# Attention and two mixture layers: the second half's products with v in two visits, three steps apart

## The chip, the cores and the metric

The kernel runs on one core of a Trainium2 chip. The core has a matrix engine (PE, which also loads its weights, PEld), a vector engine (DVE), a scalar engine (ACT), a general engine (POOL) and a queue that issues transfers (SP). Each takes its own instructions in the order in which they stand and waits for the others by semaphores. The metric is the device time of one execution in microseconds (us).

## The reference, cut to what matters

```python
def _attn_ref(q, k, v, tau):                 # 4 batches, 8 heads, 576 rows, 64 columns
    scores = scale * np.matmul(q, k.transpose(0, 1, 3, 2))
    thresh = np.max(scores, axis=-1, keepdims=True) - tau
    scores = np.where(scores >= thresh, scores, -1000000000.0)
    scores = scores - np.max(scores, axis=-1, keepdims=True)
    attn = np.exp(scores)
    attn = attn / (np.sum(attn, axis=-1, keepdims=True) + 1e-09)
    return np.matmul(attn, v)
# then h = x @ w_in, g = h * tanh(softplus(h)), x = g @ w_out      (2304 tokens, 512 -> 2048 -> 512)
# then a soft mixture of 8 experts with 4 slots each
```

The change lies in the attention alone, in its last product `attn @ v`.

## The kernel before, in words

The attention takes 16 pairs of heads, one after the other. A pair has two heads of 576 rows. Its rows come in nine chunks of 128: four of each head and a last one that holds the 64 rows left of both. The main loop runs over steps, one chunk each, so that step 9n+j works on chunk j of pair n; below, "step j" is a step of that place in any pair. PE, DVE and ACT are kept in one written order (`manual_schedule`), so that the place of a call in the loop is the place in the engine's queue.

In a step stand, in this order:

- PE, `emit_S`: the scores `s` of the chunk, 128 rows by 576 keys, four matmuls (eight in step 8, whose rows are of two heads). A score tile has two PSUM banks; there are three such tiles, so the scores of chunk i take the tile of chunk i-3 and wait for DVE to be done with that.
- PE, `emit_T`: four matmuls with the identity turn the masked exponentials `p` of the chunk three steps back (`T_LAG`), keys to the partitions, into a bank of `tp`. ACT copies the bank to `pT`. Of the name `tp` there are two banks, which the turns and the products with v share.
- DVE and ACT, `emit_E`: DVE finds the extreme `nm` of each row (its scores are negated), ACT takes the exponentials `e`.
- DVE, `emit_P`, for the chunk before: mask, product and row sum in one instruction; then `emit_th`, the next threshold.

Keys 512 to 575 are turned apart (`emit_R`, parts 0, 1 and 2 at the steps of `R_AT`): two small matmuls into the unused end of the step's score tile, ahead of the scores in PE's order; `evac_R` at the end of the step copies them to `pTr`.

A pair's product with v (`emit_V`) is done by halves of its rows: half 0 has 256 of each head, half 1 has 320. It is five key groups (kc 0 to 4) of two matmuls each, side by side in the two halves of PE's columns, summed in one bank of `tp`; kc 4 reads `pTr`. ACT then copies the bank to `xT`. `pv_at` places it: half 0 of pair n at the end of step 0 of pair n+1 (`PV_0`), half 1 at the end of step 4 of pair n+1 (`PV_1`).

Other work rides in the same loop. POOL splits the next pair's q and k. SP loads k, q and v two pairs ahead; v has three buffers. In pairs 1 to 12, three early weight tiles are unpacked: in every fourth pair (1, 5, 9) the step 4 holds an ACT instruction (`rebase`, L158), and the other parts are DVE instructions at the ends of steps 4 and 6 (`CONV`, `CVN`): one at step 6 in pairs 1, 5, 9; one at each of both steps in pairs 2, 3, 6, 7, 10, 11; one at step 4 in pairs 4, 8, 12. At step 4 of pairs 4, 8 and 12 a batch's row sums are turned too, and ACT copies them out (`rt`). At step 6 of pairs 12 to 15 ACT copies a part of the token block (`x_hi`). After the attention come the two mixture layers, which the change does not touch.

Of the kernel before, what the change touches and what calls it, by code (L numbers as in the profile page):

```python
# [8 lines left out]
F32 = mybir.dt.float32  # L9
# [15 lines left out]
NPR = B * NP  # L25
# [7 lines left out]


T_LAG = 3
PV_0 = 29
PV_1 = 14
R_AT = (6, 2, 3)
NORM_AT = (0, 4)
CONV = (4, 6, 13, 15, 22, 24, 31)  # L40
CVN = (9, 45, 81)
# [23 lines left out]
def pow2(n):  # L65

    return 1 << (n.bit_length() - 1)
# [3 lines left out]
def kernel(  # L71
# [21 lines left out]
    def copy_act(dst, src):  # L93
        act.activation(out=dst, in_=src, func=ACTF.Copy)  # L94
# [7 lines left out]
    tp = ctx.enter_context(tc.tile_pool(name="tp", bufs=2))  # L102
# [5 lines left out]
    ps_t = ph2.enter_context(tc.tile_pool(name="ps_t", bufs=2, space=PSUM))  # L108
# [75 lines left out]
    def spans(t0, n):  # L184
        a = t0
        while a < t0 + n:
            blk = a // BT
            e = min(t0 + n, (blk + 1) * BT)
            yield blk, a - blk * BT, a - t0, e - a
            a = e  # L190
# [194 lines left out]
            copy_act(tr[:64, 256:320], ps[:64, 0, :64])  # L385
            copy_act(tr[64:, 256:320], ps[64:, 1, 64:])

    def emit_V(n, half):

        b, hp = divmod(n, NP)  # L390
        w = 256 if half == 0 else 320
        t, tr = pT[n, half]
        vt, vrt = V[n]
        pv = ps_t.tile([128, 512], F32, name="tp")
        for kc in range(5):
            for h in range(2):
                hs = slice(64 * h, 64 * h + 64)
                lhsT, rhs = (vt[:, kc, h], t[:, kc, h]) if kc < 4 else (vrt[:, h], tr)
                pe.matmul(pv[hs, :w], lhsT=lhsT, rhs=rhs, start=(kc == 0), stop=(kc == 4))  # L399
        for blk, x0, p0, ln in spans(b * S + 256 * half, w):  # L400
            copy_act(xT[blk][:, hp, x0:x0 + ln], pv[:, p0:p0 + ln])

    def pv_at(i, z):

        n, k = divmod(3 * i + z, 27)
        for nn, half, place in ((n, 0, PV_0), (n - 1, 0, PV_0), (n - 1, 1, PV_1)):
            if place == k + 27 * (n - nn) - 27 * half and 0 <= nn < NPR:
                emit_V(nn, half)

    def norm_a(b):  # L410
        r = p1.tile([128, 36], F32, name="rr", bufs=2)
# [4 lines left out]
    def norm_b(b, i):  # L416
        o = SH if i < NCH else 0
        ps = st[i]["s"][:36, 0, o:o + 128]
        pe.transpose(ps, rinv[b], ident)
        return lambda: norm_out(b, ps)  # L420
# [80 lines left out]
    with tc.manual_schedule():  # L501
# [49 lines left out]
        for i in range(NCH + 9):  # L551
            n, j = divmod(i, 9)
            live = i < NCH
            if live or j in R_AT[1:]:
                st[i] = {"s": ps_s.tile([128, 2, 512], F32, name="s")}
            R = None
            pv_at(i, 0)
            if n < NPR and j == R_AT[0]:
                R = (n, 0, i)
            if n >= 1 and j in R_AT[1:]:  # L560
                R = (n - 1, R_AT.index(j), i)
            if R:
                emit_R(*R)
            turn_out = None
            if n >= 1 and (n - 1) % NP == NP - 1:
                if j == (NORM_AT[1] if n < NPR else R_AT[2]):
                    turn_out = norm_b((n - 1) // NP, i)
            if live:
                emit_S(i)
            pv_at(i, 1)  # L570
            if T_LAG <= i < NCH + T_LAG:
                emit_T(i - T_LAG)
# [4 lines left out]
            if live:  # L577
# [11 lines left out]
                for m in range(NWA):  # L589
# [3 lines left out]
                    if z in CONV:  # L593
                        cv[m][CONV.index(z)]()
                        if z == CONV[-1] and m + 1 < NWA:
                            early_w(m + 1)
            pv_at(i, 2)
            if n >= 1:
                m = n - 1
# [276 lines left out]
        for c0, w in COLS:  # L876
            n = pow2(1024 // w)
# [104 lines left out]
        for g in range(NF, NG, 2):  # L982
            blk, m = divmod(g, NF)
            prev = [g - 1] if g == NF else [g - 2, g - 1]
            plan = TRIPLES_0 if g == NF else TRIPLES_1 if m == 2 else TRIPLES
# [387 lines left out]
```

## Time and profile before

| | us |
|---|---|
| median of 3 runs (lowest to highest) | 755.63 (754.92 to 756.26) |
| the profiled execution | 755.94 |
| span of its instructions | 754.2 |
| PE busy | 728.1 (97%) |
| DVE busy | 519.9 (69%) |
| ACT busy | 459.1 (61%) |
| POOL busy | 391.9 (52%) |

The span runs from the first instruction to the last; 1.7 us of the execution lie around it. The shares are means over stages: the attention is the first 290 us, and there DVE and ACT are nearly as busy as PE. A busy PE is not PE at its peak, since the ends of matmuls are modelled; how long PE is kept by a group of instructions is read from the start of it to the start of the next.

### The profile page before, as it was taken

To read this page: it belongs to the slowest core of one execution; us is meant where nothing else is said; L and a number is where in the kernel's file an instruction comes from. 1 tells how busy PE (TensorE), PEld (TensorE's weight loads), DVE (VectorE), ACT (ScalarE), POOL (GpSimd) and SP (SyncE) were. 2 spreads that over 40 slices of the span, in tenths; PEclk is the share of its full clock that TensorE was granted. 3 is DMA by queue.
4 is the path that set the end of the run, shared out by engine and by line. 5 is a ranking of instruction groups with operands and counts; after the bars stand their busy time and mean duration, and the time that the engine had idled before them with its cause. 6 is when DMAs were issued, how large, how long until landed. Compare 5 with 4: busy or idle time off the path is not lost.

```text
span 754.2 us, 12760 instructions
## 1 busy us (share of the span) xinstructions
PE 728.1 (97%) x4641; PEld 596.0 (79%) x4641; DVE 519.9 (69%) x1018; ACT 459.1 (61%) x880; POOL 391.9 (52%) x395
## 2 busy tenths in 40 slices
PE   8999999999999999999999999999999999999995
PEld 6777777777777778998999888887898888898443
DVE  7888888888888883656986756568867545754413
ACT  6877787777777775444464655566646555644213
POOL 6665567666647733333645755465755454544000
PEclk8999999999999999999999999999999999999998
DMA  7422443433313203343330100000006111259798
GB/s 246 134 81 83 154 127 98 124 126 107 128 56 97 81 4 126 113 143 137 112 112 1 63 1 1 1 1 0 1 1 232 69 57 56 94 218 370 251 397 296
DMA packets 45678, 84.85 MB, mean 113 GB/s; under 512 B 6048, under 2 KB 21040, under 8 KB 45616
## 3 DMA queue, kind: packets, MB, share of 16 engines
q1 hardware_dynamic: 45344, 83.88, 32.8%
q8 instruction: 36, 0.59, 0.3%
q14 instruction: 26, 0.21, 0.1%
q10 hardware_dynamic: 272, 0.16, 0.1%
HBM read 79.23 MB, written 4.79 MB: 111 GB/s over the span
## 4 chain that ended last, share of the span: by engine, by line
PE 75%; DVE 13%; issue 6%; ACT 5%; DMA 1%; SPq 0%; POOL 0%; ACTq 0%
PE tp L399 11%; PE s L647 8%; PE s L649 8%; PE s L648 8%; DVE pab L340 7%; PE s L307 7%; PE tp L742 5%; PE tp L744 4%; PE tp L743 4%; PE tp L483 3%; PE tp L485 3%; PE tp L484 3%; PE tp L360 2%; PE hp L1195 2%; DVE nm L317 2%
## 5 line engine op out<-in xcount | busy, mean ns | idle before, releaser
L307 PE MATMUL s<-kb,Q 128*128 128x288 f32 (+2 forms) x672 | 126.0, 316 | 10.2 <-DVE pab L340 4.6
L317 DVE TENSOR_REDUCE nm<-s 128x1 f32<-128x576 f32 x144 | 108.0, 750 | 38.8 <-PE s L307 38.6
L307 PEld LDWEIGHTS s<-kb,Q 128*128 128x128 f32 x672 | 95.1, 192 | 37.0 <-DVE pab L340 15.5
L466 POOL TENSOR_TENSOR wo<-wr,wo 128x512 fp32r<-128x512 f32 x48 | 68.5, 1426 | 99.2 <-ACT wo L94 85.5
L318 ACT ACTIVATE e<-s,nm 128x576 f32<-128x576 f32 x144 | 106.5, 740 | 18.7 <-DVE nm L317 15.2
L647 PE MATMUL s<-wo,gg 128*128 128x512 f32 x288 | 115.8, 402 | 0.8 <-DVE big L657 0.7
L649 PE MATMUL s<-wo,gg 128*128 128x512 f32 x288 | 114.0, 396 | 0.0
L648 PE MATMUL s<-wo,gg 128*128 128x512 f32 x288 | 113.8, 395 | 0.0
L340 DVE SCALAR_TENSOR_TENSOR pab<-s,th,e 128x576 f32<-128x576 f32 x128 | 103.5, 808 | 1.7 <-ACT pTr L94 1.7
L94 ACT ACTIVATE pT<-tp 128x512 f32<-128x512 f32 x144 | 86.2, 598 | 24.6 <-PE tp L360 24.1
L360 PE MATMUL tp<-ident,pab 128*128 128x128 f32 x512 | 78.6, 276 | 0.1
L399 PE MATMUL tp<-pT,vt 128*64 128x320 f32 (+1 forms) x512 | 69.1, 412 | 0.4 <-ACT pT L94 0.3
L732 POOL TENSOR_TENSOR wi<-wr,wi 128x256 fp32r<-128x256 f32 x48 | 47.3, 986 | 41.6 <-ACT wi L94 41.5
L753 ACT ACTIVATE hs<-hs 128x384 f32<-128x384 f32 x64 | 33.4, 522 | 56.5 <-DVE hs L1031 35.7
L732 POOL TENSOR_TENSOR wi<-ev,wi 128x256 fp32r<-128x256 f32 x64 | 52.5, 831 | 23.8 <-ACT wi L94 23.8
L649 PEld LDWEIGHTS s<-wo,gg 128*128 128x128 f32 x288 | 54.4, 189 | 12.6
L360 PEld LDWEIGHTS tp<-ident,pab 128*128 128x128 f32 x512 | 62.2, 142 | 0.8 <-issue 0.7
L647 PEld LDWEIGHTS s<-wo,gg 128*128 128x128 f32 x288 | 54.5, 189 | 9.8 <-issue 1.8
L648 PEld LDWEIGHTS s<-wo,gg 128*128 128x128 f32 x288 | 54.6, 190 | 7.5 <-POOL wo L466 0.4
L756 DVE TENSOR_TENSOR gg<-hs,gg 128x384 fp32r<-128x384 f32 x64 | 54.5, 852 | 7.6 <-ACT gg L94 7.6
L91 POOL TENSOR_SCALAR kb<-kr,kscale 128x576 fp32r<-128x576 f32 x30 | 22.5, 750 | 61.6 <-PE s L307 61.6
L399 PEld LDWEIGHTS tp<-pT,vt 128*64 128x64 f32 x512 | 33.9, 136 | 24.9 <-issue 5.1
(284 smaller groups left out, 1572.0 us busy)
## 6 DMA issues: line engine op xcount, KB each, us to landing
kr<-in_k SPq DMA_DIRECT2D x32, 288.0 KB, 3.0
qr<-in_q SPq DMA_DIRECT2D x32, 288.0 KB, 3.2
big<-in_w SPq DMA_DIRECT2D x15, 512.0 KB, 7.1
wr<-in_w SPq DMA_DIRECT2D x14, 512.0 KB, 3.3
big<-in_w_in SPq DMA_DIRECT2D x10, 512.0 KB, 4.8
big<-in_w_out SPq DMA_DIRECT2D x10, 512.0 KB, 5.0
wr<-in_w SPq DMA_DIRECT2D x13, 352.0 KB, 8.3
big<-in_w SPq DMA_DIRECT2D x13, 320.0 KB, 6.9
```

The source lines that it names most:

```text
L94: act.activation(out=dst, in_=src, func=ACTF.Copy)
L307: pe.matmul(s[:, f, a:z], lhsT=t[:, o:o + 128], rhs=kb[:, hh, ko:ko + z - a], start=(j == 0), stop=(j == len(plan) - 1 and z == SH),)
L317: dve.tensor_reduce(out=nm, in_=s, axis=AX.XY, op=ALU.min)
L318: act.activation(out=e, in_=s, func=ACTF.Exp, bias=nm[:, 0:1], scale=-1.0)
L340: dve.scalar_tensor_tensor(out=p.rearrange("p (a b) -> p a b", a=2), in0=d["s"][:, :, :SH], scalar=d["th"][:, 0:1], in1=d["e"], op0=ALU.is ...
L360: pe.transpose(ps[:, kc], p[:, ko:ko + 128], ident)
L399: pe.matmul(pv[hs, :w], lhsT=lhsT, rhs=rhs, start=(kc == 0), stop=(kc == 4))
L466: pool.tensor_tensor(out=t[:, 1], in0=src, in1=t[:, 0].bitcast(F32), op=ALU.subtract)
L647: pe.matmul(ps, lhsT=hi[:, ts], rhs=w[:, 0], start=(m == 0), stop=False)
L648: pe.matmul(ps, lhsT=hi[:, ts], rhs=w[:, 1], start=False, stop=False)
L649: pe.matmul(ps, lhsT=lo[:, ts], rhs=w[:, 0], start=False, stop=(m == NF - 1))
L732: pool.tensor_tensor(out=lo, in0=src, in1=hi.bitcast(F32), op=ALU.subtract)
```

## The change

Half 0's product stays at step 0. Half 1's is now done in two visits: kc 0 and 1 at the end of step 3, kc 2, 3 and 4 at the end of step 6. In between the sum stays in its bank of `tp`. Part 2 of `emit_R`, which kc 4 needs, moves from step 3 to step 5. The counts and shapes of all instructions are the same.

```diff
 T_LAG = 3
-PV_0 = 29
-PV_1 = 14
-R_AT = (6, 2, 3)
+PV = ({29: (0, 1, 2, 3, 4)}, {38: (0, 1), 47: (2, 3, 4)})
+R_AT = (6, 2, 5)
...
-    def emit_V(n, half):
+    pvs = {}
+
+    def emit_V(n, half, kcs):
...
-        pv = ps_t.tile([128, 512], F32, name="tp")
-        for kc in range(5):
+        if kcs[0] == 0:
+            pvs[half] = ps_t.tile([128, 512], F32, name="tp")
+        pv = pvs[half]
+        for kc in kcs:
             for h in range(2):
...
                 pe.matmul(pv[hs, :w], lhsT=lhsT, rhs=rhs, start=(kc == 0), stop=(kc == 4))
+        if kcs[-1] < 4:
+            return
         for blk, x0, p0, ln in spans(b * S + 256 * half, w):
             copy_act(xT[blk][:, hp, x0:x0 + ln], pv[:, p0:p0 + ln])
...
-        for nn, half, place in ((n, 0, PV_0), (n - 1, 0, PV_0), (n - 1, 1, PV_1)):
-            if place == k + 27 * (n - nn) - 27 * half and 0 <= nn < NPR:
-                emit_V(nn, half)
+        for half, plan in enumerate(PV):
+            for back in range(2):
+                if k + 27 * back in plan and 0 <= n - back < NPR:
+                    emit_V(n - back, half, plan[k + 27 * back])
```

PE, steps 2 to 5 of the second pair before (`tp_953` is the bank of the product, the other `tp` those of turns, `s` with `pr` or `pab` the small turns of `emit_R`):

```order
L360 MATMUL tp_889<-ident_88,pr_108 128x128 x4
L377 MATMUL s_903<-ident_88,pr_108 128x128 x2
L307 MATMUL s_903<-kb_643,Q1_1_110 128x288 x2
L307 MATMUL s_903<-kb_643,Q2_1_112 128x288 x2
L360 MATMUL tp_912<-ident_88,pab_873 128x128 x4
L307 MATMUL s_931<-kb_643,Q1_1_110 128x288 x2
...
L360 MATMUL tp_936<-ident_88,pab_873 128x128 x4
L399 MATMUL tp_953<-pT1_779,vt_355 64x320 x8
L399 MATMUL tp_953<-pTr1_780,vrt_356 64x320 x2
L307 MATMUL s_965<-kb_643,Q1_1_110 128x288 x2
...
L360 MATMUL tp_970<-ident_88,pab_922 128x128 x4
```

PE, steps 3 to 7 of the same pair in the changed kernel, where `tp_927` is the product's bank:

```order
L359 MATMUL tp_910<-ident_88,pab_873 128x128 x4
L403 MATMUL tp_927<-pT1_779,vt_355 64x320 x4
L306 MATMUL s_932<-kb_643,Q1_1_110 128x288 x2
...
L359 MATMUL tp_937<-ident_88,pab_873 128x128 x4
L376 MATMUL s_954<-ident_88,pr_108 128x128 x2
...
L359 MATMUL tp_961<-ident_88,pab_920 128x128 x4
L374 MATMUL s_979<-ident_88,pab_873 128x128
...
L359 MATMUL tp_986<-ident_88,pab_920 128x128 x4
L403 MATMUL tp_927<-pT1_779,vt_355 64x320 x4
L403 MATMUL tp_927<-pTr1_780,vrt_356 64x320 x2
L306 MATMUL s_1008<-kb_643,Q1_1_110 128x288 x2
...
L359 MATMUL tp_1015<-ident_88,pab_971 128x128 x4
```

Eight matmuls and two stood together between two steps; now four stand behind the turn of step 3 and six behind that of step 6. Before, the turns go through the two banks by turns. In the changed kernel the product holds one bank from step 3 to step 6, and the five turns of steps 3 to 7 (`tp_910`, `tp_937`, `tp_961`, `tp_986`, `tp_1015`) are all placed in the other.

ACT, steps 3 to 5 of that pair before (`e` are the exponentials, `pT` the copies of turns, `big` the copy of the product):

```order
L94 ACTIVATE pT0_910<-tp_912 128x4x128
L318 ACTIVATE e_919<-s_903,nm_918 128x576
L94 ACTIVATE pTr1_780<-s_903 64x64 x2
L94 ACTIVATE pT0_910<-tp_936 128x4x128
L318 ACTIVATE e_943<-s_931,nm_942 128x576
L94 ACTIVATE big_105<-tp_953 128x320
L94 ACTIVATE pT0_910<-tp_970 128x4x128
L318 ACTIVATE e_977<-s_965,nm_976 128x576
```

ACT, steps 3 to 7 of that pair in the changed kernel:

```order
L93 ACTIVATE pT0_908<-tp_910 128x4x128
L317 ACTIVATE e_917<-s_903,nm_916 128x576
L93 ACTIVATE pT0_908<-tp_937 128x4x128
L317 ACTIVATE e_944<-s_932,nm_943 128x576
L93 ACTIVATE pT0_908<-tp_961 128x4x128
L317 ACTIVATE e_968<-s_954,nm_967 128x576
L93 ACTIVATE pTr1_780<-s_954 64x64 x2
L93 ACTIVATE pT0_908<-tp_986 128x4x128
L317 ACTIVATE e_993<-s_979,nm_992 128x576
L93 ACTIVATE big_105<-tp_927 128x320
L93 ACTIVATE pTr0_909<-s_979 128x256
L93 ACTIVATE pT1_1013<-tp_1015 128x4x128
```

The copy of part 2 (`pTr1_780`, 64x64) went from behind the exponentials of step 3 to behind those of step 5, the copy of the product from step 4 to step 6. Each copy of a turn still stands behind the exponentials of the step before.

## Rows read from the trace of the kernel before

**Rows 1.** Busy time by engine in the stretch of pairs 1 to 14; columns as printed.
```profile
core 0: us, PE busy (x) PEld busy (x) DVE busy (x) ACT busy (x) POOL busy (x), PEclk, DMA share, GB/s
21.70:264.22 242.52, 234.52 (x1743) 180.82 (x1741) 206.28 (x529) 186.63 (x355) 158.83 (x158) 1.00 0.34 108
```
**Rows 2.** Who waited for whom, same stretch: total us, times, longest us.
```profile
DVE nm L317 <- PE s L307: 35.1, 28, 1.7
```
**Rows 3.** Timeline (start us, us): first reduction of pairs 1 to 5 and 15.
```profile
21.70 0.75 DVE L317 TENSOR_REDUCE nm<-s 128x1 f32<-128x576 f32 x1
38.98 0.74 DVE L317 TENSOR_REDUCE nm<-s 128x1 f32<-128x576 f32 x1
56.45 0.75 DVE L317 TENSOR_REDUCE nm<-s 128x1 f32<-128x576 f32 x1
73.92 0.75 DVE L317 TENSOR_REDUCE nm<-s 128x1 f32<-128x576 f32 x1
90.83 0.75 DVE L317 TENSOR_REDUCE nm<-s 128x1 f32<-128x576 f32 x1
264.22 0.75 DVE L317 TENSOR_REDUCE nm<-s 128x1 f32<-128x576 f32 x1
```
**Rows 4.** Timeline of PE in pair 8, from half 0's product at step 0.
```profile
142.75 1.95 PE L399 MATMUL tp<-pT,vt 128*64 128x256 f32 x16
...
145.06 0.80 PE L307 MATMUL s<-kb,Q 128*128 128x288 f32 x4
145.70 0.60 PE L360 MATMUL tp<-ident,pab 128*128 128x128 f32 x4
146.13 0.38 PE L375 MATMUL s<-ident,pab 128*128 128x128 f32 x2
146.27 0.78 PE L307 MATMUL s<-kb,Q 128*128 128x288 f32 x4
...
147.44 0.44 PE L377 MATMUL s<-ident,pr 128*128 128x128 f32 x2
147.64 0.78 PE L307 MATMUL s<-kb,Q 128*128 128x288 f32 x4
...
149.63 0.60 PE L360 MATMUL tp<-ident,pab 128*128 128x128 f32 x4
150.16 2.37 PE L399 MATMUL tp<-pT,vt 128*64 128x320 f32 x16
...
153.00 0.80 PE L307 MATMUL s<-kb,Q 128*128 128x288 f32 x4
...
155.39 0.41 PE L307 MATMUL s<-kb,Q 128*128 128x288 f32 x1
```
**Rows 5.** Timeline of DVE in pair 8, at steps 1, 5 and 6.
```profile
145.90 0.76 DVE L317 TENSOR_REDUCE nm<-s 128x1 f32<-128x576 f32 x1 [0.69 <-PE s L307]
...
153.84 0.76 DVE L317 TENSOR_REDUCE nm<-s 128x1 f32<-128x576 f32 x1 [1.16 <-PE s L307]
154.52 0.81 DVE L340 SCALAR_TENSOR_TENSOR pab<-s,th,e 128x576 f32<-128x576 f32 x1
...
155.38 0.75 DVE L317 TENSOR_REDUCE nm<-s 128x1 f32<-128x576 f32 x1
```
**Rows 6.** Timeline of ACT in pair 8: a turn's copy, exponentials, small copies.
```profile
146.33 0.60 ACT L94 ACTIVATE pT<-tp 128x512 f32<-128x512 f32 x1 [0.71 <-PE tp L360]
146.83 0.73 ACT L318 ACTIVATE e<-s,nm 128x576 f32<-128x576 f32 x1
...
150.44 0.43 ACT L94 ACTIVATE pTr<-s 64x64 f32<-64x64 f32 x2
...
153.45 0.26 ACT L94 ACTIVATE rt<-s 36x128 f32<-36x128 f32 x1
```
**Rows 7.** Timeline of ACT: the weight tile's part in pair 5, `x_hi` in pair 15.
```profile
99.86 1.17 ACT L158 ACTIVATE big<-big 128x1024 f32<-128x1024 f32 x1
...
278.42 0.84 ACT L94 ACTIVATE big<-big 128x768 fp32r<-128x768 f32 x1
```

## The prediction

> **What bounds the kernel now.** I first read the windows view of pairs 1 to 14: in 242.52 us PE is busy for 234.52, DVE for 206.28, ACT for 186.63, at a granted clock of 1.00, the upper of PE's two levels, 2.4 GHz [rows 1]. All three are near the bound, so shares do not say which wait counts. The list of waits does: DVE waits 28 times, twice per pair, for scores, 35.1 us in all [rows 2], and those are the only long waits between PE and DVE. The timeline of one pair shows where: DVE stands still 0.69 us at step 1, behind half 0's product, and 1.16 us at step 5, behind half 1's [rows 5]. In the other steps DVE runs at 1.54 us from reduction to reduction (153.84 to 155.38 [rows 5]), and PE is the one held up: a step of scores and turn keeps PE about 1.07 us (0.63 + 0.44 below), but scores cannot run ahead by more than three tiles. So PE loses time before a product, and DVE loses it behind one. The length of a pair is the last fact needed: 17.28, 17.47, 17.47 and 16.91 us in pairs 1 to 4 [rows 3]; pairs 1, 2 and 3 carry a DVE part of a weight tile at step 6, pair 4 does not. So that part costs 0.37 (pair 1) or 0.56 us there, in full.
>
> **The times of PE, start to start** [rows 4]. Scores to turn 0.64 and 0.63 (I use 0.63; the scores of step 8, with twice the matmuls, 1.26). Turn to small turns 0.43, to a product 0.53, to scores 0.44 (estimate, from the 0.43). Small turns to scores 0.14, part 2 0.20. Half 0's product 2.31, half 1's 2.84: five key groups, 0.57 each, so the first visit is 1.14 and the second 1.70. From a score's start to its reduction 0.84 (153.00 [rows 4] to 153.84 [rows 5]). Scores of step i wait until the masking in step i-2 has ended: 1.55 behind the reduction there (153.84 to the score start at 155.39 [rows 4, 5]). On ACT: a turn's copy starts 0.63 behind the turn and takes 0.60; exponentials start 0.93 behind their reduction and take 0.73; the two small copies of part 2 take 0.43, the row sums' copy 0.26 [rows 4 to 6]. PE starts 0.06 behind what it waits for (masking from 154.52 for 0.81, scores at 155.39 [rows 4, 5]).
>
> **A walk through a pair of before**, from the start of step 1's scores (0), without other work. S is scores, T turn, N reduction. N1 0.84. T1 0.63, S2 1.20, T2 1.83. Part 2 waits for the masking until 0.84 + 1.55 = 2.39 (trace 147.44 - 145.06 = 2.38 [rows 4]), S3 2.59, T3 3.22. S4 waits for N2 + 1.55 = 3.93. T4 4.56, product 5.09 to 7.93, where S5 starts (trace 7.94 [rows 4]). T5 8.56, S6 9.13. N5 is 8.77, so S7 waits until 10.32 (trace 10.33), S8 until N6 + 1.55 = 11.86. T8 13.12, S0 13.56, T0 14.19, product 14.72 to 17.03. Pair 4 lasts 16.91 [rows 3]: the walk is 0.12 long.
>
> **The same walk with the change.** Part 2 no longer stands at step 3: S3 2.39, T3 3.02, first visit 3.55 to 4.69 = S4. DVE would have been ready for it at 0.84 + 3 x 1.54 = 5.46, and N4 is 4.69 + 0.84 = 5.53: 1.14 us of product now cost DVE 0.07. T4 5.32, part 2 5.75, S5 5.95, T5 6.58. The small turns of step 6 wait for N4 + 1.55 = 7.08, S6 7.22, T6 7.85, second visit 8.38 to 10.08 = S7. N7 is 10.92 against 10.15 at DVE's pace (N4 + 3 x 1.54): 0.77 idle. T7 10.71, S8 11.15, T8 12.41, S0 12.85, T0 13.48, half 0's product 14.01 to 16.32. A pair without other work comes to 16.32 against 17.03: 0.71 less. PE's work is the same; what goes is its waiting at S4, S7, S8, since it now arrives there later with part of the product done.
>
> **What the one bank costs.** The turns of steps 4 to 7 now wait for ACT to have copied the turn before, and that copy stands behind the exponentials of the step before. T5 needs T4's copy, which ends at 5.95 + 0.60 = 6.55: 6.61 against 6.58. T6 needs T5's copy: exponentials of step 4 end at 5.53 + 0.93 + 0.73 = 7.19, T5's copy is ready to start at 7.21 and ends at 7.81: 7.87 against 7.85. So I price the bank at 0.03 per pair, below the 0.12 by which the walk is off, but with no room: any ACT work put in front of T5's copy delays PE in full. The trace of before has no turn that waits for the bank of the turn just ahead, so its cost is bounded from the rows: at least nothing, at most copy, wait and exponentials one behind the other (rival 2). The Trainium skill, "Perfetto Trace Analysis", section "Optimizing Tensor Performance", says that independent matmul groups should rotate through different PSUM banks, so that the evacuation of one overlaps the matmuls of the next. That speaks against this change; no run here yet shows several turns in one bank, and by that rule the time would be that of rival 1 or 2.
>
> **Other edits.** Part 2's copies end at 7.08 + 0.93 + 0.73 + 0.43 = 9.17 (N5 is 5.95 + 0.84, but at DVE's pace 7.07), and key group 4 starts at 8.38 + 1.14 = 9.52: hidden, with 0.30 to spare. The product's copy on ACT comes two steps later; nothing reads it in the attention's next steps, and the bank is free again for the turn of step 8. The buffer of v of the pair before is read until step 6 instead of 4; on SP the next v waits behind it, and the loads of row sums behind that, which POOL uses five steps later: 5 x 1.54 us cover them.
>
> **Pairs with other work.** Three of four early pairs differ from the plain 16.32.
> - Pairs 1, 5, 9: ACT's part of a weight tile (1.17 [rows 7]) stands behind the exponentials of step 4, ahead of T5's copy. That copy starts at 7.19 + 1.17 = 8.36 and ends at 8.96, T6 starts at 9.02 instead of 7.85: 17.49. The DVE part at step 6 falls into the idle time there. Before 17.28: a loss.
> - Pairs 2, 6, 10: a DVE part of 0.56 at step 4 moves N5 to 7.63, part 2's copies to 9.72 and key group 4 to 9.77 for 9.52: 16.57. The part at step 6 is hidden by the 0.77.
> - Pairs 3, 7, 11: the 0.37 part at step 4: key group 4 at 9.58 for 9.52, 16.38.
> - Pairs 4, 8, 12: the 0.56 at step 4, and the row sums' copy of 0.26 ahead of T5's copy: T6 0.26 later, which also covers key group 4: 16.58.
> - Pairs 13, 14: the block copy (0.84 [rows 7]) now falls behind the second visit, where DVE's next masking is later than the exponentials: 16.32. It could cost up to 0.84.
>
> **Sum.** 3 x (17.49 + 16.57 + 16.38 + 16.58) + 2 x 16.32 = 233.70 against 242.52 [rows 1, 3]: 8.82 less. If the walk is 0.12 long after as before, 14 x 0.12 = 1.7 more: 10.5. Pair 15 is cut short by the end of the attention and has two more weight copies on ACT: 0 to 0.7, I take 0.3. The last pair's product only fills PE between other matmuls: 0. So 9.1 to 10.8, I take 10.0. The profiled execution took 755.94, the median of the runs is 755.63, 0.3 below it: 755.6 - 10.0 = 745.6. What comes after the attention is bound by PE and moves up as a whole.
>
> **Rivals.**
> 1. The bank gives part of it back. Each 0.1 us by which T5's or T4's copy ends later than I worked out is 0.1 on PE in 15 pairs, 1.5 us. At 0.33 a pair, half is gone: 751. At 0.65 all: 755.6. For it: no room at T5 and T6, and ACT has 187 of 243 us of work. Against: copies in the trace start within 0.63 of their turn wherever ACT is free [rows 4, 6].
> 2. Slower: ACT and PE fall into lockstep at steps 4 to 7: turn 0.63, copy 0.60, wait 0.06, and exponentials 0.73 that come only then, 2.02 per step against 1.54, four times: 1.9 a pair, 28 in all, less the 10 gained: 774. It decides from 0.65 a pair. Against: exponentials hang on the reduction, not on the turn, and run while PE does scores and turn.
> 3. Faster still: the weight tile's part on ACT does not delay T5's copy in pairs 1, 5, 9 (3 x 1.17 = 3.5): 742. Against: ACT takes its work in order.
>
> That both visits are done as described is seen from the order of instructions, so this is no case.
>
> **How the numbers follow.** Forecast 0.70 (gain of 6 to 13 us), rival 3 0.07, rival 1 0.14 (0.09 with something left, 0.05 with nothing), rival 2 0.09. Faster by over 0.2% (1.5 us, about what can be told from no change) is 0.70 + 0.07 + 0.09 = 0.86; the same 0.05; slower 0.09. The range goes from rival 3's 742 to rival 1's half at 751.
>
> **What would show it.** Right: two waits of DVE for scores per pair, at steps 1 and 7, that at step 5 gone; a pair without other work near 16.2 to 16.3 us; 17.4 in pairs 1, 5, 9, with PE waiting there for ACT before the turn of step 6; the attention some 10 us shorter and all behind it as it was. Wrong: PE waits of some tenths before the turns of steps 4 to 7 in every pair, or before key group 4.

## The result, and the profile after

The changed kernel takes 745.57 us (median of 4 runs, 744.88 to 746.07), the kernel before beside it 755.79. The ratio is 0.9865, with a 95% interval of 0.9848 to 0.9883. Run once more it took 745.38 against 755.39, ratio 0.9888 (0.9867 to 0.9910). So it is faster, by 8.5 to 10.2 us by the two ratios; the forecast was 745.6. The profiled execution took 745.62, its span is 743.8.

The windows view of the kernel after, pairs 1 to 14 (answers to [rows 1]):

```profile
21.10:255.51 234.41, 232.01 (x1741) 177.42 (x1739) 208.60 (x529) 185.57 (x354) 158.97 (x159) 1.00 0.36 112
```

The same 14 pairs take 234.41 us instead of 242.52: 8.11 less, with nearly the same busy time on DVE (208.60 for 206.28) and ACT (185.57 for 186.63). The list of waits in that stretch (answers to [rows 2]); the last two rows are of PE's weight loads, which stand ahead of their matmuls and show PE's waits:

```profile
DVE nm L316 <- PE s L306: 22.7, 22, 1.4
...
PEld tp L359 <- ACT pT L93: 6.5, 25, 1.0
...
PEld tp L403 <- ACT pTr L93: 3.7, 8, 0.7
```

DVE waits 22.7 us for scores instead of 35.1. New are PE's waits for ACT: 25 times before a turn, for the copy of the turn before (1.0 us the longest), and 8 times before key group 4, for part 2's copies. PE's waits for masking, which the change was to take away, are seen in the same way, first before and then after:

```profile
PEld s L307 <- DVE pab L340: 13.9, 39, 0.5
```

```profile
PEld s L306 <- DVE pab L339: 2.7, 14, 0.2
```

The 39 are nearly three a pair; the 14 left are one a pair, at S3 (in the walk step 3 waits for masking before and after). The first reductions of pairs 1 to 5 and 15 (answers to [rows 3]):

```profile
21.10 0.75 DVE L316 TENSOR_REDUCE nm<-s 128x1 f32<-128x576 f32 x1
38.35 0.74 DVE L316 TENSOR_REDUCE nm<-s 128x1 f32<-128x576 f32 x1
54.91 0.75 DVE L316 TENSOR_REDUCE nm<-s 128x1 f32<-128x576 f32 x1
71.28 0.75 DVE L316 TENSOR_REDUCE nm<-s 128x1 f32<-128x576 f32 x1
87.80 0.75 DVE L316 TENSOR_REDUCE nm<-s 128x1 f32<-128x576 f32 x1
255.51 0.75 DVE L316 TENSOR_REDUCE nm<-s 128x1 f32<-128x576 f32 x1
```

Pairs 1 to 4 last 17.25, 16.56, 16.37 and 16.52 us; they lasted 17.28, 17.47, 17.47 and 16.91. A timeline of PE in pair 13, which has no part of a weight tile, from the start of step 1's scores:

```profile
224.65 0.80 PE L306 MATMUL s<-kb,Q 128*128 128x288 f32 x4
...
228.20 1.30 PE L403 MATMUL tp<-pT,vt 128*64 128x320 f32 x8
229.42 0.80 PE L306 MATMUL s<-kb,Q 128*128 128x288 f32 x4
...
230.63 0.77 PE L306 MATMUL s<-kb,Q 128*128 128x288 f32 x4
231.35 0.66 PE L359 MATMUL tp<-ident,pab 128*128 128x128 f32 x4
231.84 0.40 PE L374 MATMUL s<-ident,pab 128*128 128x128 f32 x2
232.00 0.77 PE L306 MATMUL s<-kb,Q 128*128 128x288 f32 x4
232.70 0.66 PE L359 MATMUL tp<-ident,pab 128*128 128x128 f32 x4
233.28 1.30 PE L403 MATMUL tp<-pT,vt 128*64 128x320 f32 x8
234.41 0.71 PE L403 MATMUL tp<-pTr,vrt 128*64 128x320 f32 x4
235.05 0.80 PE L306 MATMUL s<-kb,Q 128*128 128x288 f32 x4
```

The walk had the first visit at 3.55 and S4 at 4.69; here they are 3.55 and 4.77. It had T5, T6, the second visit and S7 at 6.58, 7.85, 8.38 and 10.08; here they are 6.70, 8.05, 8.63 and 10.40. So the order of events is as walked, and each visit and each waiting turn is a little dearer: T5 stands 0.72 behind S5 and T6 0.70 behind S6, where the walk has 0.63. The DVE of this pair waits at step 7:

```profile
235.88 0.76 DVE L316 TENSOR_REDUCE nm<-s 128x1 f32<-128x576 f32 x1 [0.95 <-PE s L306]
```

In pair 5, which holds ACT's part of a weight tile at step 4, the timeline of ACT shows this part ahead of T5's copy:

```profile
97.09 1.15 ACT L157 ACTIVATE big<-big 128x1024 f32<-128x1024 f32 x1
98.14 0.58 ACT L93 ACTIVATE pT<-tp 128x512 f32<-128x512 f32 x1
```

and that of PE the turn of step 6, which waits for this copy:

```profile
98.78 0.66 PE L359 MATMUL tp<-ident,pab 128*128 128x128 f32 x4 [0.72 <-ACT pT L93]
```

Not all of the difference of the two spans (754.2 and 743.8) is the change. The products behind the attention are the same work in both, but in the profiled execution of before PE's granted clock was at its lower level for a part of that stretch. Its windows rows, ahead of pair 1 and of those products, and the rows of after for the same work:

```profile
0.00:21.70 21.70, 17.96 (x87) 15.14 (x89) 17.28 (x49) 14.18 (x23) 14.16 (x21) 0.84 0.67 219
417.87:451.58 33.71, 31.86 (x151) 28.24 (x150) 22.48 (x35) 19.35 (x44) 20.11 (x23) 0.95 0.07 23
```

```profile
0.00:21.10 21.10, 17.57 (x87) 14.47 (x89) 17.09 (x48) 13.90 (x23) 13.59 (x20) 0.92 0.69 225
408.65:440.84 32.19, 30.32 (x152) 27.03 (x150) 22.51 (x35) 19.33 (x44) 20.11 (x23) 1.00 0.08 24
```

That is 1.5 us in the products, at a mean granted clock of 0.95 against 1.00. The 0.6 us ahead of pair 1 stand at 0.84 against 0.92, but the clock does not explain them: before_parts reaches pair 1 at 21.72 us with a clock of 1.00 in that stretch. Their cause is open. The products' low stretch is no effect of the split: of the kernels with the split, the traces of after_parts and act_part_at_8 show it (0.95), that of after_again does not (1.00).

The mean granted clock of a whole execution says the same of the medians. Beside after_again, five executions of the kernel before at 0.990 took 755.35 to 756.06 us, and two of the changed kernel at 0.989 and 0.990 took 747.63 and 747.86; one of each, at 0.997 and 0.996, took 753.14 and 745.38. At an equal clock the change is worth some 8 us there, an estimate from few executions.

### The profile page after: what moved, and what is told of

Same layout as the page of the kernel before. It is cut to its first block, busy times and chain, and to the rows that moved or that the text cites. A ratio compares the mean times of both kernels' runs of the same rounds, so it can differ in the third digit from the quotient of the medians.

```text
span 743.8 us, 12760 instructions
## 1 busy us (share of the span) xinstructions
PE 723.8 (97%) x4641; PEld 590.4 (79%) x4641; DVE 522.0 (70%) x1018; ACT 457.9 (62%) x880; POOL 391.3 (53%) x395
## 4 chain that ended last, share of the span: by engine, by line
PE 88%; ACT 5%; DVE 4%; issue 2%; DMA 1%; SPq 0%; POOL 0%; ACTq 0%
PE s L306 12%; PE tp L403 11%; PE s L654 8%; PE s L656 8%; PE s L655 8%; PE tp L359 8%; PE tp L749 5%; PE tp L751 5%; PE tp L750 4%; PE tp L490 3%; PE tp L492 3%; PE tp L491 3%; PE hp L1202 2%; PE so L1234 2%; PE tp L789 1%
## 5 line engine op out<-in xcount | busy, mean ns | idle before, releaser
L359 PE MATMUL tp<-ident,pab 128*128 128x128 f32 x512 | 80.1, 280 | 2.2 <-ACT pT L93 2.2
L403 PE MATMUL tp<-pT,vt 128*64 128x320 f32 (+1 forms) x512 | 72.7, 415 | 0.3 <-ACT pT L93 0.3
L359 PEld LDWEIGHTS tp<-ident,pab 128*128 128x128 f32 x512 | 59.8, 141 | 7.7 <-ACT pT L93 6.7
L93 ACT ACTIVATE wi<-wr 128x256 fp32r<-128x256 f32 (+1 forms) x63 | 29.3, 465 | 38.4 <-DVE wr L168 23.3
```

The source lines that it names most:

```text
L359: pe.transpose(ps[:, kc], p[:, ko:ko + 128], ident)
```

## The experiments

Nine runs follow, each with the kernel before beside it for its ratio. Lengths of pairs are differences of first reductions in their traces.

**after_parts**: the weight tiles' parts moved away from step 4.

```diff
-CONV = (4, 6, 13, 15, 22, 24, 31)
+CONV = (-1, 0, 6, 9, 15, 18, 24)
-                    if z == 0 and m == 0:
+                    if z == CONV[0] and m == 0:
```

> The changed kernel, with the weight tiles' parts moved: ACT's part to step 8 of the pair before, DVE's parts to steps 0 and 6, where DVE waits for scores. Theory (PE is now the bound, and what pairs lose beside it is ACT work ahead of a turn's copy and DVE work ahead of key group 4): every pair of 1 to 12 comes to 16.3 to 16.5 us, no PE wait of 1 us before the turn of step 6 is left, 14 pairs in about 230 us instead of 234.4, so 740.5 to 742. Rival (the one bank itself holds the turns back in every pair): pairs stay at 16.5 to 17 us, 744 to 746.

742.09 us, ratio 0.9838 (0.9825 to 0.9850), at the upper end of what was expected: faster than the kernel before, and by the traces than the changed kernel. The windows view of pairs 1 to 14:

```profile
21.67:252.49 230.82, 230.82 (x1741) 178.11 (x1739) 207.94 (x530) 186.28 (x354) 160.10 (x158) 1.00 0.36 114
```

Pairs 1 to 14 all last 16.4 to 16.6 us, and by this view PE is busy through the whole stretch: what the parts cost in the changed kernel was 3.6 us. The rival falls by its time (744 to 746). In small, though, it is there: a pair without other work is 16.48, not the 16.32 of the walk, and the list of waits still has 20 waits before turns, 3.4 us, none over 0.2.

**before_parts**: the kernel before, parts moved to where it waits.

```diff
-CONV = (4, 6, 13, 15, 22, 24, 31)
+CONV = (-1, 0, 4, 9, 13, 18, 22)
-                    if z == 0 and m == 0:
+                    if z == CONV[0] and m == 0:
```

> The kernel before, with the parts moved in the same way, DVE's to steps 0 and 4, where it waits there. Theory (each part at step 6 cost its own time): pairs 1 to 3 come to the 16.9 us of pair 4, 238 us for 14 pairs instead of 242.5, so about 751. With the run above this gives the gain of the two visits alone: 0.5 to 0.7 us in each of 15 pairs, 8 to 10.5 us. Rival (the two visits gained mostly by hiding the parts of step 6): the two kernels with moved parts differ by under 5 us.

750.69 us, ratio 0.9951 (0.9939 to 0.9963), as the theory had it.

```profile
21.72:260.25 238.53, 232.39 (x1743) 180.51 (x1741) 212.26 (x530) 185.88 (x355) 162.90 (x158) 1.00 0.35 110
```

Pairs 1 to 11 last 16.94 to 16.97. With the parts out of the way of either kernel the two visits are worth 750.69 - 742.09 = 8.6 us (the rival, under 5, falls), 238.53 - 230.82 = 7.7 of it in these pairs: 0.48 in a pair without other work (16.96 to 16.48), not the 0.71 of the walk. Pairs 12 to 14 gain 0.8 to 0.9, since there the block copy's delay goes too.

**whole_at_6**: half 1's product whole at step 6.

```diff
-PV = ({29: (0, 1, 2, 3, 4)}, {38: (0, 1), 47: (2, 3, 4)})
+PV = ({29: (0, 1, 2, 3, 4)}, {47: (0, 1, 2, 3, 4)})
```

> The changed kernel with half 1's product whole, all five key groups at step 6, part 2 at step 5; no bank is held over steps. Theory (it is the split that lets PE arrive at S4, S7 and S8 without waiting): one long wait of DVE of about 1.9 us less the parts hidden in it, pairs of about 17.3 us, 754 to 757, no gain over before. Rival (the later place, which hides the parts of step 4 and 6, does it): 748 to 751.

754.14 us, ratio 0.9994 (0.9985 to 1.0003). Its timeline of DVE in pair 13, the reduction of step 7:

```profile
243.78 0.76 DVE L316 TENSOR_REDUCE nm<-s 128x1 f32<-128x576 f32 x1 [1.91 <-PE s L306]
```

One wait of 1.91 us as expected, and no gain. The later place does hide the parts (pair 2 lasts 17.21 for 17.47), but pairs with little else lose as much (pair 4: 17.23 for 16.91). So it is the split, not the later place. The whole product at step 3, where the first visit stands, and other cuts than two and three key groups were not run.

**part2_at_3**: part 2 of the small turns back at step 3.

```diff
-R_AT = (6, 2, 5)
+R_AT = (6, 2, 3)
```

> The changed kernel with part 2 of the small turns back at step 3. Theory (walk): the first visit, and all of PE behind it, starts 0.2 us later; pairs are 0.2 to 0.25 us longer, except 2, 6 and 10, in which key group 4 no longer waits: 2 to 3 us in all, 747.5 to 749. Rival (the place of part 2 does not matter, the split does all): within 1 us of 745.6. Other rival (key group 4's wait is what is left to gain): faster, 743 to 744.

747.07 us, ratio 0.9904 (0.9891 to 0.9916), against 0.9865 and 0.9888 of the changed kernel; with the second of these the intervals overlap, and the traces decide. DVE in pair 13, step 4:

```profile
232.41 0.76 DVE L316 TENSOR_REDUCE nm<-s 128x1 f32<-128x576 f32 x1 [0.29 <-PE s L306]
```

It waits 0.29, and the reduction comes 1.89 behind that of step 3 instead of 1.71 in the changed kernel; plain pairs are 0.18 longer (16.59 and 16.65 for 16.40 and 16.48); 14 pairs take 1.7 us more. The exceptions were not those expected: pair 2 loses like the others, while pairs 6, 7, 8, 10 and 11 change by less than 0.1. The move of part 2 is a small, real share of the gain, a little under the 2 to 3 us expected.

**after_act4** and **before_act4**: one more ACT copy at step 4, in either kernel.

```diff
+    spare_act = p1.tile([128, 4, 128], F32, name="spare_act")
...
+                if n >= 1 and j == 4:
+                    act.activation(out=spare_act, in_=ident.unsqueeze(1).to_broadcast([128, 4, 128]), func=ACTF.Copy)
```

> The changed kernel with one more ACT instruction in each of pairs 1 to 15: a copy of the identity, 128x512, about 0.6 us, into a tile that nobody reads, behind the exponentials of step 4. Theory (T5's copy has no room, and T6 waits for it in the one bank): 0.5 to 0.6 us longer in pairs with nothing else there, 0.2 to 0.5 where DVE's parts make key group 4 wait anyway, 5.5 to 8 us in all, 751 to 753.5. Rival (ACT has room, the bank does not matter): within 1 us of 745.6.

> The kernel before with the same additional ACT instruction in the same place, where ACT waits for the product and the turns alternate between two banks. Theory: hidden, within 1 us of the kernel before. Rival (ACT as a whole is near the bound of a pair, with or without the one bank): 3 us or more slower.

750.26 us, ratio 0.9940 (0.9928 to 0.9952), and 755.45, ratio 1.0004 (0.9993 to 1.0016). In the kernel before it costs nothing that can be measured; in the changed one about 5 us, 4.1 of it in pairs 1 to 14; 750.26 lies a little under the 751 to 753.5 expected. Timeline of ACT in pair 13 of after_act4:

```profile
236.03 0.63 ACT L598 ACTIVATE spare_act<-ident 128x512 f32<-128x512 f32 x1
236.55 0.60 ACT L93 ACTIVATE pT<-tp 128x512 f32<-128x512 f32 x1
```

and PE there:

```profile
237.20 0.66 PE L360 MATMUL tp<-ident,pab 128*128 128x128 f32 x4 [0.21 <-ACT pT L93]
```

The turn of step 6 waits for the copy that the new instruction has pushed back. Pair 13 is 0.29 longer, not 0.5 to 0.6: in a pair with nothing else ACT did have some room, so the size expected was too high by half, the mechanism right. Where ACT's weight part already stands there (pairs 1, 5, 9) the copy costs 0.50 to 0.54; where key group 4 waits longest (pairs 6 and 10) it costs nothing. before_act4 differs from after_act4 in two things, the two banks and ACT's idle time before the product at that place, and does not part them.

**after_again** and **act_part_at_8**: the changed kernel once more, and with ACT's part of the weight tiles alone moved.

```diff
-CONV = (4, 6, 13, 15, 22, 24, 31)
+CONV = (-1, 6, 13, 15, 22, 24, 31)
-                    if z == 0 and m == 0:
+                    if z == CONV[0] and m == 0:
```

> The changed kernel once more, on the chip of the two runs beside it. 8.5 to 10.5 us under the kernel before: the pairs gave 8.1 in the traces, pair 15 another 1.1 less 0.6 after it, and the rest of the 10.3 between the two profiled spans should be differences of the granted clock between single executions.

> The changed kernel with only ACT's part of the weight tiles moved, from step 4 of pairs 1, 5 and 9 to step 8 of the pair before. Theory (in the one bank ACT's 1.17 us at step 4 goes to PE in full): pairs 1, 5 and 9 from 17.25 to about 16.45 us, all else as it was, 2.4 us less than the changed kernel. Rival (the DVE parts at step 4 make up the difference to the run with all parts moved): under 1 us less.

745.38 us, ratio 0.9888 (0.9867 to 0.9910), 10.0 under the kernel before; and 744.46, ratio 0.9860 (0.9843 to 0.9876). The medians differ by 0.9, the ratios by 0.28%, 2.1 us; the intervals overlap, so the times alone leave the size open. The traces settle it: pairs 1, 5 and 9 go from 17.25, 17.29 and 17.28 to 16.44, 16.48 and 16.48, the others change by under 0.1, the 14 pairs take 2.2 us less (2.4 were expected), and the wait before turns has lost its long ones (list of waits of act_part_at_8):

```profile
PEld tp L359 <- ACT pT L93: 4.3, 26, 0.2
```

**half0_split**: after_parts with half 0's product in two visits too.

```diff
-PV = ({29: (0, 1, 2, 3, 4)}, {38: (0, 1), 47: (2, 3, 4)})
+PV = ({26: (0, 1), 29: (2, 3, 4)}, {38: (0, 1), 47: (2, 3, 4)})
```

> The changed kernel with all parts moved, and half 0's product in two visits too: key groups 0 and 1 at the end of step 8, 2 to 4 at the end of step 0. Theory (PE never waits long any more, so DVE's wait of 1.3 us at step 1 is no loss): no gain, two more entries and turns that share a bank cost 0.1 to 0.25 a pair, 743.5 to 746. Rival (every wait of DVE behind a product is worth splitting): 5 us or more faster than the run with parts moved, under 737.

747.43 us, ratio 0.9903 (0.9887 to 0.9919), 5.3 us above after_parts, which ran on another chip. That is beyond the 746 expected. The windows view of pairs 1 to 14, 4.8 us more than after_parts:

```profile
21.70:257.32 235.62, 235.62 (x1741) 177.15 (x1740) 209.02 (x528) 186.08 (x353) 159.57 (x158) 1.00 0.36 111
```

PE from the end of pair 5 into pair 6: the first visit, behind the turn of step 8, the scores and the turn of step 0, and the second visit:

```profile
103.39 0.66 PE L359 MATMUL tp<-ident,pab 128*128 128x128 f32 x4
103.97 1.08 PE L403 MATMUL tp<-pT,vt 128*64 128x256 f32 x8
104.98 0.79 PE L306 MATMUL s<-kb,Q 128*128 128x288 f32 x4
105.62 0.60 PE L359 MATMUL tp<-ident,pab 128*128 128x128 f32 x4
106.14 1.08 PE L403 MATMUL tp<-pT,vt 128*64 128x256 f32 x8
107.06 0.60 PE L403 MATMUL tp<-pTr,vrt 128*64 128x256 f32 x4
107.59 0.79 PE L306 MATMUL s<-kb,Q 128*128 128x288 f32 x4
```

By the windows view PE is busy throughout, so DVE's wait behind half 0's product was no loss, as the theory said, and the rival falls. The loss was larger than expected: pairs last 16.82 for 16.48. Of the 0.34, 0.09 is the first visit itself (1.01 to the next scores, where two fifths of 2.31 are 0.92), 0.06 the second (1.45, where three fifths are 1.39), 0.17 that a turn is now followed by a product (0.58) instead of scores (0.41). The turns next to it do not wait. So here one more entry into a product costs PE a third of a microsecond.

## Why the prediction was right

The sign and the mechanism were right: PE's waits for masking at S4, S7 and S8 go, and the split does it. That the time was met to 0.1 us is luck. Pairs 1 to 14 gave 8.1 us, less than the 8.8 to 10.5 forecast, and pair 15 with what follows it 0.5 (1.1 less 0.6) for 0.3, so the traces show 8.6 us for the 10.0 of the sum, as the two kernels with moved parts do. The rest lies outside the sum: 1.5 us of the two profiled spans' difference went with the granted clock behind the attention, and the 755.6 that the forecast starts from is high for the kernel before, which had medians of 754.37, 754.81 and 755.39 beside the experiments.

| term | forecast, us | measured, us |
|---|---|---|
| pairs 1, 5, 9 | 17.49 | 17.25, 17.30, 17.27 |
| pairs 2, 6, 10 | 16.57 | 16.56, 16.81, 16.96 |
| pairs 3, 7, 11 | 16.38 | 16.37, 16.46, 16.59 |
| pairs 4, 8, 12 | 16.58 | 16.52, 16.63, 16.81 |
| pairs 13, 14 | 16.32 | 16.40, 16.48 |
| gain of pairs 1 to 14 | 8.8 to 10.5 | 8.1 |

- **DVE behind the first visit**: the reductions of steps 3 and 4 were to be 1.61 us apart (N4 5.53 less 0.84 + 2 x 1.54) and are 1.71; the wait at step 5 is gone, that at step 7 is 0.95 in pair 13 for 0.77. Right.
- **A pair without other work** was to gain 0.71 and gained 0.48 (before_parts against after_parts): the walk of before was 0.07 too long (17.03 for 16.96), that of the change 0.16 too short (16.32 for 16.48). Two of its terms were too small. One is the second entry: I added 0.09 for it (turn to product 0.53 instead of turn to scores 0.44), but the visits themselves are dearer too, in pair 13 1.22 instead of 1.14 and 1.77 instead of 1.70. half0_split gives the price of one more entry for half 0, 0.34. The other is the bank.
- **The bank** was priced at 0.03. In pair 13 it cost about 0.15: T5 and T6 stand 0.72 and 0.70 behind their scores for 0.63. What follows a turn that has waited comes later too, by 0.49 instead of 0.43 and 0.58 instead of 0.53. By its own signs of being wrong the prediction was so in small, since every pair has short waits before these turns and eight pairs wait before key group 4. That it left no room and that ACT work there delays PE in full was too strong: after_act4 and act_part_at_8 show that ACT work ahead of T5's copy goes to PE, but 0.29 of 0.63 and 0.8 of 1.15 us, while before_act4 shows that it did not before. For this the Trainium skill's rule in "Perfetto Trace Analysis", section "Optimizing Tensor Performance", that independent matmul groups should rotate through different PSUM banks, names the right danger. The trace agrees that turns in one bank wait for the copy: before there are no such waits, and with five turns in one bank the weight loads ahead of turns wait for 4.3 us in 14 pairs, 0.3 a pair, and never over 0.2 (act_part_at_8). The times of rivals 1 and 2, which the prediction took from the rule, did not come: the 0.48 that the split gives is what is left after these waits.
- **Pairs 1, 5, 9** were to lose by ACT's part and did not lose, but did not gain either: 17.25 to 17.30 against 17.28. The part costs such a pair 0.8 us (17.25 against 16.44 with it moved), not 1.17; ACT's instructions overlap at their ends (the copy starts 1.05 behind a part of 1.15), and a plain pair's T6 already comes at 8.05, not 7.85. Right in kind, oversized.
- **Key group 4** was to wait 0.25 in pairs 2, 6 and 10 and waits up to 0.7, and in pairs 4, 7, 8, 11 and 12 as well. The price of 0.56 that I read from step 6 holds at step 4 in pair 2 (the reductions of steps 4 and 5 are 2.13 apart for 1.53, 0.60 more), but not in pairs 6 and 10 (0.84 and 1.00 more), where DVE's part takes longer (below).
- **Pair 15** was to give 0.3; to the last reduction it gave 1.1. What lies between that and the next layer's products lost 0.6, where I had 0; why, no run shows.

Rival 2 fell: there is no lockstep. Rival 1 came true in small, at 0.15 a pair, under half of the 0.33 at which it takes half of the gain. Rival 3 did not come: the part does delay T5's copy. act_part_at_8 shows what it would have given, 2.2 us, by moving the part.

## What to carry to other kernels

Where two engines take turns at being late, a long block on one of them can cost by what the buffers between cannot hold. Here cutting one in two pieces gave 0.48 us a pair; cutting a second one, when PE no longer waited long, lost 0.34, since each piece has its own entry price. Cut until the engine that runs the block no longer waits, and no further; which sizes of piece are best was not tried. Then re-place whatever had been hidden in the old wait: here moving the parts of three weight tiles gave the 14 pairs another 3.6 us. Before a buffer is held longer, look for the instruction that sits one place ahead of the copy which frees the other.

## What was not expected of the hardware

The same DVE instruction on 128x512 words takes 0.68 us in pair 2 and 0.92 in pair 6 (1.07 in pair 10). DVE in pairs 2 and 6 of the changed kernel:

```profile
47.60 0.68 DVE L163 SCALAR_TENSOR_TENSOR big<-big 128x512 uint32<-128x512 uint32 x1
...
114.36 0.92 DVE L163 SCALAR_TENSOR_TENSOR big<-big 128x512 uint32<-128x512 uint32 x1
```

POOL at those places:

```profile
46.58 0.75 POOL L90 TENSOR_SCALAR ks<-kr,kscale 128x576 f32<-128x576 f32 x1
...
113.31 1.42 POOL L237 TENSOR_TENSOR Q<-qr,Q 128x576 fp32r<-128x576 f32 x1
114.71 1.18 POOL L90 TENSOR_SCALAR ks<-kr,kscale 128x576 f32<-128x576 f32 x1
```

In pair 2 POOL's copy ends before the DVE instruction starts. In pair 6 the DVE instruction starts while POOL's TENSOR_TENSOR, which has two inputs, still runs, and ends 0.55 us behind its end; in pairs 8 and 10 it ends 0.54 and 0.55 behind it. POOL's copy, which follows, is longer too. In pair 8 of the kernel before, POOL's copy but for 0.03 us stands alone beside a DVE instruction of this kind:

```profile
152.01 0.68 DVE L169 SCALAR_TENSOR_TENSOR wr<-big 128x512 uint32<-128x512 uint32 x1
...
152.02 1.28 POOL L91 TENSOR_SCALAR ks<-kr,kscale 128x576 f32<-128x576 f32 x1
```

There the DVE instruction takes its 0.68, and the copy 1.28. So the rows suggest that POOL's TENSOR_TENSOR holds up the DVE instruction, and that the DVE instruction lengthens POOL's copy; it was not tried by itself, and spans on POOL are rough. The kernel before had the same (0.88 in pair 6), but hidden in DVE's wait.
